# Splitting the value weights earlier in the opening of a one-core attention and gated-feed-forward kernel

## The chip, the core and the metric

The kernel runs on one core of one Trainium2 chip. The metric is device time in microseconds (us) of one launch: 689.45 us before the change, the median of three runs (689.45 to 689.49).

The engines are named as the profile names them. PE is the matrix engine (PEld is its weight load, which runs beside the matmuls), DVE the vector engine, ACT the scalar engine, POOL the general-purpose engine, and SP the engine that issues nearly all loads and stores.

## The reference, cut to what matters

`x` holds 2048 tokens of 448 channels. All weight products use the layer-normed tokens `xn`:

```python
xn = _layernorm(x, axis=-1)
return x + _A_ref(xn, A_wq, A_wk, A_wv, A_wo, A_beta) + _B_ref(xn, B_w_gate, B_w_up, B_w_down)
```

`_A_ref` is attention with 16 heads of 28 channels over four segments of 512 tokens. It projects queries, keys and values (`xn @ wq`, `xn @ wk`, `xn @ wv`), attends causally inside a segment, mixes in a read of a memory that is summed over the earlier segments, and multiplies by `wo`. `_B_ref` is `(sigmoid(xn @ w_gate) * (xn @ w_up)) @ w_down` with 1792 inner channels. What the change touches is only the very beginning: the layer norm of the first 512 tokens and the product `xn @ wv` for them.

## The kernel before, in words

**Precision.** Every operand of a large product is split into a high part, rounded to the matmul type by an ACT copy, and a low part, which is the rest. The low part of weights in the opening is made by POOL, and that of tokens by DVE. One product is a sum of eleven matmuls over pairs of parts.

**Blocks and tiles.** The 2048 tokens stand in four blocks of 512, and a block in four tiles of 128. `acc[b]` holds the raw tokens of a block; `xs[b]` holds the normed tokens turned (channels on partitions): parts 0 to 2 are the high parts of three groups of 128 channels, part 3 has the last 64 channels, high in one half and low in the other, and parts 4 to 6 are the low parts. So that part 3 can hold both, the last 64 channels are repeated in columns 448 to 511 of the normed tile `xn`; in the first block ACT makes these repeated channels (L324). `wv[0]` to `wv[3]` are the high value weights, `wv[4]` to `wv[7]` the low ones.

**The opening (L407 to L501).** For each of the first four tiles, the same steps follow each other:

- `statistics`: three DVE instructions, mean and variance (L294 to L296).
- `root`: one small ACT square root (L301).
- `normalised`: on DVE a reciprocal, two small corrections (L308 to L311) and the normed tile (L320), then the repeated channels on ACT (L324).
- `turn_high`: four PE transposes (L95) into a PSUM bank and one ACT copy into the high parts (L97). The first three transposes need only L320; the fourth also reads the repeated channels.
- `turn_low`: two DVE subtractions that make the low parts (L102, L103).

Beside them, `split_v(t)` makes `wv[t]` by an ACT copy of the raw weights (L431) and `wv[4 + t]` by a POOL subtraction (L432). `value_terms(b, t, pv, terms, n0, n1)` issues the matmuls n0 to n1 of the eleven of one tile (L335), and `store_values` copies the sum out of PSUM on ACT (L339). `fill(n)` issues n small matmuls of no use but to keep PE busy (L445), each of which the trace counts as two; ten more of them (L442) stand at the very start.

`EARLY[0]`, the order of the eleven matmuls for the first two tiles, begins with three high by high (they need `wv[0]`, `wv[1]` and `wv[2]`), then three with the tokens' low parts, then one with part 3 and `wv[3]`, then three with `wv[4]` to `wv[6]`, and last the one with `wv[7]`.

**What sets the order.** Around the opening stands

```python
with tc.tile_pool(name="front", bufs=2) as sb, tc.manual_schedule(engines=FRONT):
```

with PE, ACT and DVE in `FRONT`: the instructions of these three engines run in just the order in which the code lists them. POOL and SP are ordered by the framework. Each engine takes its instructions in order; one that waits holds back all behind it. SP issues the loads in this order: tokens of tile 0 (L409), of tile 1 (L410), first half of the value weights (L411, `wv[0]` and `wv[1]`), second half (L412, `wv[2]` and `wv[3]`), tokens of tiles 2 and 3 together (L413), then weights of queries and keys and the next block's tokens.

After the opening come the queries and keys of each block (L355), the memory updates, and the long part in which feed-forward matmuls and attention alternate in an order written out by hand for PE and SP.

Of the kernel before, what the change touches and what calls it, by code (L numbers as in the profile page):

```python
# [17 lines left out]
D = 448  # L18
# [33 lines left out]
EARLY = [HIGH + LOW_X + [(3, 3)] + LOW_W + [(3, 7)], HIGH + LOW_W + LOW_X + [(3, 3), (3, 7)]]  # L52
# [9 lines left out]
def kernel(  # L62
# [28 lines left out]
    def transpose_high(pt, src, dst, t):  # L91

        tok = slice(t * P, (t + 1) * P)
        for c in range(4):
            T.transpose(pt[:, c * P:(c + 1) * P], src[:, c * P:(c + 1) * P], ident)  # L95
        p3 = pt.rearrange("p (c n) -> p c n", c=4)
        A.activation(dst[:, 0:4, tok], p3, AF.Copy)  # L97
        return p3

    def transpose_low(p3, dst, t):  # L100
        tok = slice(t * P, (t + 1) * P)
        V.tensor_sub(dst[:, 4:7, tok], p3[:, 0:3], dst[:, 0:3, tok].bitcast(F32))  # L102
        V.tensor_sub(dst[64:, 3, tok], p3[64:, 3], dst[64:, 3, tok].bitcast(F32))  # L103
# [11 lines left out]
    def bank(name, tag):  # L115
        return ps.tile([P, L], F32, name=name, tag=tag, bufs=banks[tag])
# [32 lines left out]
    def four_k(dtype, name):  # L149
        return mid.tile([P, 2, L], dtype, name=name, tag="4k", bufs=4)  # L150
# [125 lines left out]
    with tc.tile_pool(name="front", bufs=2) as sb, tc.manual_schedule(engines=FRONT):  # L276
# [11 lines left out]
        def statistics(b, t0, steps):  # L288

            stats = sb.tile([P, steps, 6], F32, name=f"stats{steps}")  # L290
            mv = sb.tile([P, steps, 2], F32, name=f"mv{steps}")
            vh = sb.tile([P, steps], F32, name=f"vh{steps}")
            for t in range(steps):
                V.bn_stats(stats[:, t, :], acc[b][:, t0 + t, :])  # L294
                V.bn_aggr(mv[:, t, :], stats[:, t, :])
            V.tensor_scalar(vh, mv[:, :, 1], EPS, -0.5, op0=ALU.add, op1=ALU.mult)  # L296
            return mv, vh

        def root(vh):
            y = sb.tile([P, vh.shape[1]], F32, name=f"y{vh.shape[1]}")  # L300
            A.activation(y, vh, AF.Sqrt, scale=-2.0)  # L301
            return y

        def rstd(mv, vh, y):

            steps = vh.shape[1]
            tm = sb.tile([P, steps], F32, name=f"tm{steps}")
            V.reciprocal(y, y)  # L308
            if steps == 1:
                V.tensor_scalar(tm, y, y, vh, op0=ALU.mult, op1=ALU.mult)  # L310
                V.tensor_scalar(y, tm, 1.5, y, op0=ALU.add, op1=ALU.mult)  # L311
            else:
                V.tensor_mul(tm, y, y)
                V.tensor_mul(tm, tm, vh)
                V.scalar_tensor_tensor(y, tm, 1.5, y, op0=ALU.add, op1=ALU.mult)
            return [(mv[:, t, 0:1], y[:, t:t + 1]) for t in range(steps)]

        def normalise(b, t, mean, y):
            xn = sb.tile([P, 512], F32, name="xn")
            V.tensor_scalar(xn[:, :D].rearrange("p (m h c) -> p h m c", h=H, c=4),  # L320
                              acc[b][:, t, :].rearrange("p (h m c) -> p h m c", h=H, c=4), mean, y,
                              op0=ALU.subtract, op1=ALU.mult)
            if b == 0:
                A.activation(xn[:, D:], xn[:, 384:D], AF.Copy)  # L324
            else:
                G.tensor_copy(xn[:, D:], xn[:, 384:D])
            return xn
# [4 lines left out]
        def value_terms(b, t, pv, terms, n0=0, n1=len(TERMS)):  # L332
            for n in range(n0, n1):
                a, w = terms[n]
                T.matmul(pv[:, :D], xs[b][:, a, t * P:(t + 1) * P], wv[w],  # L335
                         start=n == 0, stop=n == len(TERMS) - 1)

        def store_values(b, t, pv):
            A.activation(vst[:, t, :, :DH], pv[:, :D].rearrange("p (h d) -> p h d", d=DH), AF.Copy)  # L339
            if t == NT - 1:  # L340
                nc.sync.dma_start(vd[b], vst.rearrange("p t h d -> p t (h d)"))
# [65 lines left out]
        raw = [four_k(F32, "wv_raw") for _ in range(2)]  # L407
        raw = [r.rearrange("p a n -> p (a n)")[:, :2 * D] for r in raw]
# [2 lines left out]
        nc.sync.dma_start(raw[0], w_v[:, :2 * D])  # L411
        nc.sync.dma_start(raw[1], w_v[:, 2 * D:])  # L412
        nc.sync.dma_start(acc[0][:, 2:4, :], x[2 * P:L, :].rearrange("(t p) d -> p t d", p=P))  # L413
        raw = [raw[t // 2][:, t % 2 * D:(t % 2 + 1) * D] for t in range(4)]
        nc.sync.dma_start(stage[:, 0:2, :], w_qk[0:2].rearrange("c p n -> p c n"))
        nc.sync.dma_start(stage[:, 2:4, :], w_qk[2:4].rearrange("c p n -> p c n"))
        raw_qk = [stage[:, c, :] for c in range(4)]
# [8 lines left out]
                nc.sync.dma_start(gate[32 * j:32 * j + 32], beta[j::HG].partition_broadcast(32))  # L426
        G.memset(vst[:, :, :, DH:], 1.0)
        A.activation(gate_n, vst[:, 0, :NG, DH], AF.Sqrt)

        def split_v(t):  # L430
            A.activation(wv[t], raw[t], AF.Copy)  # L431
            G.tensor_sub(wv[4 + t], raw[t], wv[t].bitcast(F32))  # L432
# [10 lines left out]
        def fill(n):  # L443
            for _ in range(n):
                T.matmul(warm[:, :P], ident, ident, start=True, stop=True)  # L445

        def turn_high(t):
            p3[t] = transpose_high(bank("pt", "s"), xn[t], xs[0], t)

        def turn_low(t):  # L450
            transpose_low(p3[t], xs[0], t)

        def normalised(t):
            xn[t] = normalise(0, t, *rstd(*st[t], y[t])[0])
# [2 lines left out]
        st[0] = statistics(0, 0, 1)  # L457
        y[0] = root(st[0][1])
        normalised(0)
        st[1] = statistics(0, 1, 1)  # L460
        y[1] = root(st[1][1])
        turn_high(0)
        fill(5)
        split_v(0)
        split_v(1)
        normalised(1)
        split_v(2)
        split_v(3)
        turn_low(0)
        turn_high(1)  # L470
        st[2] = statistics(0, 2, 1)
        y[2] = root(st[2][1])
        turn_low(1)
        normalised(2)
        st[3] = statistics(0, 3, 1)
        pv = [bank("pv", "p") for _ in range(2)]
        for t in range(2):
            value_terms(0, t, pv[t], EARLY[0], 0, 7)
        value_terms(0, 0, pv[0], EARLY[0], 7)
        store_values(0, 0, pv[0])  # L480
        y[3] = root(st[3][1])
        turn_high(2)
        value_terms(0, 1, pv[1], EARLY[0], 7)
        store_values(0, 1, pv[1])
# [3 lines left out]
        pv = bank("pv", "p")  # L488
# [345 lines left out]
```

## Time and profile before

| what | value |
|---|---|
| median of three runs | 689.45 us (689.45 to 689.49) |
| the profiled execution's own time | 689.46 us |
| its span, first to last instruction | 687.7 us |
| PE busy | 681.7 us, 99% of the span |
| DVE busy | 567.4 us, 83% |
| ACT busy | 342.6 us, 50% |
| POOL busy | 151.3 us, 22% |

The profile is of one execution. A row of the timeline gives the start in us from the span's start, the duration in us, the engine, the line in the kernel, the operation and what it writes and reads; "x4" at its end says that four neighbouring instructions were merged, and the duration then goes from the first start to the last end. A row of the chain of waits names the work that, followed back from the end, was late at that time. Matmuls are pipelined, so several overlap, and a busy PE is not PE at its peak.

### The profile page before, as it was taken

How to read it: one execution, taken by the hardware profiler on the slowest of the kernel's cores; microseconds unless marked ns; L12 is line 12 of the kernel's file. 1: busy time of each engine (PE TensorE's matmuls, PEld its weight loads, DVE VectorE, ACT ScalarE, POOL GpSimd, SP SyncE). 2: the span in 40 equal slices, each digit the busy share in tenths (PEclk: the TensorE clock that was granted, in tenths of full speed). 3: DMA queues.
4: the chain of work that ended last, by engine and by line, in shares of the span. 5: the costliest groups of instructions: out<-in, count | busy, mean ns of one | idle time of the engine just before them, and what ended most of it. 6: DMA issues, size and time to landing. Idle time of an engine off the chain costs nothing.

```text
span 687.7 us, 10438 instructions
## 1 busy us (share of the span) xinstructions
PE 681.7 (99%) x3594; PEld 566.6 (82%) x3594; DVE 567.4 (83%) x994; ACT 342.6 (50%) x563; POOL 151.3 (22%) x349
## 2 busy tenths in 40 slices
PE   8999999999999999999999999999999999999997
PEld 7898888778878787787878878787787878878897
DVE  6765795767788988998898989989898899889863
ACT  4837555343554555543655446454653565446320
POOL 3500020101223222232332222322322322222000
PEclk9999999999999999999999999999999999999999
DMA  7446556696233323243223252314333332423342
GB/s 267 181 150 238 198 214 242 249 330 174 71 94 92 80 86 86 56 128 112 56 64 107 57 141 56 109 47 116 82 94 77 96 71 64 95 79 95 95 153 106
DMA packets 45796, 84.37 MB, mean 123 GB/s; under 512 B 6320, under 2 KB 20400, under 8 KB 45232
## 3 DMA queue, kind: packets, MB, share of 16 engines
q1 hardware_dynamic: 42736, 76.37, 35.8%
q0 software_dynamic: 3008, 7.34, 4.9%
q8 instruction: 28, 0.46, 0.3%
q14 instruction: 24, 0.20, 0.1%
HBM read 51.05 MB, written 32.64 MB: 122 GB/s over the span
## 4 chain that ended last, share of the span: by engine, by line
PE 70%; DVE 14%; issue 9%; POOL 4%; DMA 1%; ACT 1%; SPq 0%; POOLq 0%; ACTq 0%
PE pgu L247 26%; PE pd L173 13%; PE pp L355 10%; PE po L771 5%; PE pv L335 5%; PE st L612 3%; PE pa L687 3%; DVE mx L629 3%; DVE w L666 2%; POOL w L627 2%; DVE acc L174 2%; PE pmm L383 2%; PE n L401 2%; DVE hh L259 1%; DVE mx L633 1%
## 5 line engine op out<-in xcount | busy, mean ns | idle before, releaser
L247 PE MATMUL pgu<-xs,wgu 128*128 128x512 f32 x1232 | 304.1, 394 | 0.0
L247 PEld LDWEIGHTS pgu<-xs,wgu 128*128 128x128 f32 x1232 | 228.2, 188 | 47.4 <-issue 2.2
L173 PE MATMUL pd<-wdn,hh 128*128 128x448 f32 x672 | 156.0, 367 | 0.0
L627 POOL TENSOR_SCALAR_AFFINE_SELECT w<-w 128x256 f32<-128x256 f32 (+1 forms) x160 | 81.2, 509 | 236.4 <-ACT w L616 183.6
L173 PEld LDWEIGHTS pd<-wdn,hh 128*128 128x128 f32 x672 | 122.5, 188 | 12.3 <-issue 0.6
L667 ACT ACTIVATE w<-w 128x1024 f32<-128x1024 f32 (+1 forms) x96 | 87.3, 915 | 65.0 <-DVE w L666 64.2
L666 DVE TENSOR_TENSOR w<-w,mb 128x1024 f32<-128x1024 f32 (+1 forms) x96 | 98.9, 1045 | 0.1
L616 ACT ACTIVATE w<-st 128x512 f32<-128x512 f32 x128 | 74.9, 590 | 45.3 <-PE st L612 44.9
L629 DVE TRANSPOSE_TENSOR_REDUCE mx<-w 128x32 f32<-128x1024 f32 x64 | 79.0, 1235 | 17.0 <-POOL w L627 17.0
L355 PE MATMUL pp<-xs,wqk 128*128 128x512 f32 x308 | 77.7, 401 | 0.0
L174 DVE TENSOR_TENSOR acc<-pd,acc 128x448 f32<-128x448 f32 x112 | 67.1, 599 | 1.2 <-PE pd L173 1.1
L355 PEld LDWEIGHTS pp<-xs,wqk 128*128 128x128 f32 x308 | 56.8, 188 | 13.4 <-issue 2.4
L258 ACT ACTIVATE hh<-sg 128x512 fp32r<-128x512 f32 x56 | 35.2, 628 | 56.4 <-DVE sg L256 49.3
L612 PE MATMUL st<-qk 84*128 84x128 f32 (+3 forms) x256 | 61.9, 312 | 0.0
L255 ACT ACTIVATE sg<-pgu 128x512 f32<-128x512 f32 x56 | 33.2, 594 | 49.4 <-PE pgu L247 49.2
L612 PEld LDWEIGHTS st<-qk 84*128 84x128 f32 x256 | 47.6, 189 | 6.9 <-ACT w L616 0.3
L656 DVE STREAM_TRANSPOSE mb<-top 128x1024 f32<-128x1024 f32 x32 | 39.8, 1242 | 10.5 <-POOL top L653 10.1
L362 DVE TENSOR_TENSOR qk<-pp,qk 128x512 fp32r<-128x512 f32 x28 | 19.3, 688 | 29.8 <-ACT e L360 23.7
L259 DVE SCALAR_TENSOR_TENSOR hh<-sg,hh 128x512 fp32r<-128x512 f32 x56 | 38.7, 691 | 2.6 <-ACT hh L258 2.4
L335 PE MATMUL pv<-wv,xs 128*128 128x448 f32 x176 | 39.6, 376 | 0.4 <-DVE xs L102 0.3
L687 PE MATMUL pa<-w,vv 128*32 128x128 f32 (+3 forms) x512 | 39.7, 436 | 0.2
L256 DVE SCALAR_TENSOR_TENSOR sg<-sg,pgu 128x512 f32<-128x512 f32 x56 | 37.3, 665 | 1.8 <-PE pgu L247 1.6
(100 smaller groups left out, 640.6 us busy)
## 6 DMA issues: line engine op xcount, KB each, us to landing
qk<-qd SPq DMA_DIRECT2D x192, 112.0 KB
qd<-qk SPq DMA_DIRECT2D x28, 512.0 KB
raw<-in_w_ffn SPq DMA_DIRECT2D x14, 512.0 KB
vd<-vst SPq DMA_DIRECT2D x4, 1024.0 KB
vv<-vd SPq DMA_DIRECT2D x16, 256.0 KB
od<-w POOLq DMA_DIRECT2D x16, 256.0 KB, 3.8
sums<-od SPq DMA_DIRECT2D x32, 128.0 KB
out<-acc SPq DMA_DIRECT2D x16, 224.0 KB
```

The costliest lines, as they stand in the source:

```text
L173: T.matmul(pd[:, :D], l, r, start=n == 0, stop=n == len(mms) - 1)
L174: V.tensor_add(acc[b][:, t, :], pd[:, :D], acc[b][:, t, :])
L247: T.matmul(dst, wgu[f][:, w, side * P:(side + 1) * P], xs[b][:, a, :], start=n == 0, stop=n == len(TERMS) - 1)
L335: T.matmul(pv[:, :D], xs[b][:, a, t * P:(t + 1) * P], wv[w], start=n == 0, stop=n == len(TERMS) - 1)
L355: T.matmul(pp, wqk[c][:, w, :], xs[b][:, a, :], start=n == 0, stop=n == len(TERMS) - 1)
L612: T.matmul(st[:, at:at + L - kb * P], self.qk[:KS, 1, h, kb * P:(kb + 1) * P], self.qk[:KS, 0, h, kb * P:], start=True, stop=True)
L616: A.activation(w, st, AF.Copy)
L627: G.affine_select(d, d, pattern=pattern, base=0, channel_multiplier=-1, compare_op=ALU.is_ge, fill=MASK)
L629: V.tensor_reduce(mx[:, 16 * (n - 1):16 * (n + 1)], w3[:, n // 2, :2 * L].rearrange("p (b n) -> p b n", n=32), axis=mybir.AxisListType.X, ...
L666: V.tensor_sub(w, w, m)
L667: A.activation(w, w, AF.Exp, scale=SCALE)
L687: T.matmul(pa[32 * j:32 * j + 32, kb * P:], self.vv[:, kb, 32 * j:32 * j + 32], self.pairs[j // 2].block(j % 2, kb), start=kb == 0, stop=k ...
```

## The change

All lines stand in the opening. The split of the first value weights (`split_v(0)`) goes to just behind the first tile's normed tokens and repeated channels, ahead of the second tile's square root. `split_v(1)` and `split_v(2)` go ahead of the second tile's norm. Three of the first tile's value matmuls go ahead of the second tile's transposes, with two fill matmuls behind them where there were five ahead of them. The remaining matmuls of the first two tiles are dealt out anew between the turns of the second and the third tile. The two PSUM banks for them are taken earlier. The line that names the four slices of the raw weights moves, which issues nothing; loads stay as they are.

```diff
         st[0] = statistics(0, 0, 1)
         y[0] = root(st[0][1])
         normalised(0)
+        split_v(0)
         st[1] = statistics(0, 1, 1)
         y[1] = root(st[1][1])
         turn_high(0)
-        fill(5)
-        split_v(0)
         split_v(1)
+        pv = [bank("pv", "p") for _ in range(2)]
+        split_v(2)
+        value_terms(0, 0, pv[0], EARLY[0], 0, 3)
+        fill(2)
         normalised(1)
-        split_v(2)
         split_v(3)
         turn_low(0)
         turn_high(1)
         st[2] = statistics(0, 2, 1)
         y[2] = root(st[2][1])
+        value_terms(0, 0, pv[0], EARLY[0], 3, 10)
         turn_low(1)
         normalised(2)
+        value_terms(0, 1, pv[1], EARLY[0], 0, 3)
+        value_terms(0, 0, pv[0], EARLY[0], 10)
+        store_values(0, 0, pv[0])
         st[3] = statistics(0, 3, 1)
-        pv = [bank("pv", "p") for _ in range(2)]
-        for t in range(2):
-            value_terms(0, t, pv[t], EARLY[0], 0, 7)
-        value_terms(0, 0, pv[0], EARLY[0], 7)
-        store_values(0, 0, pv[0])
         y[3] = root(st[3][1])
+        value_terms(0, 1, pv[1], EARLY[0], 3, 7)
         turn_high(2)
         value_terms(0, 1, pv[1], EARLY[0], 7)
         store_values(0, 1, pv[1])
```

More of the change, by code (lines that the diff above doesn't have):

```diff
@@ L413 @@
         nc.sync.dma_start(acc[0][:, 2:4, :], x[2 * P:L, :].rearrange("(t p) d -> p t d", p=P))
-        raw = [raw[t // 2][:, t % 2 * D:(t % 2 + 1) * D] for t in range(4)]
         nc.sync.dma_start(stage[:, 0:2, :], w_qk[0:2].rearrange("c p n -> p c n"))
@@ L428 @@
         A.activation(gate_n, vst[:, 0, :NG, DH], AF.Sqrt)
+        raw = [raw[t // 2][:, t % 2 * D:(t % 2 + 1) * D] for t in range(4)]
         def split_v(t):
```

## The prediction, made before the changed kernel was run

> **What bounds the kernel now.** I read the page first, then PE's waits, then the chain of waits for the opening, and last each engine's timeline there. In the table of PE's waits the columns are the wait's total in us, how often, and the longest.
>
> ```profile
> span 687.7 us, 10438 instructions
> PE 681.7 (99%) x3594; PEld 566.6 (82%) x3594; DVE 567.4 (83%) x994; ACT 342.6 (50%) x563; POOL 151.3 (22%) x349
> ```
>
> ```profile
> PE warm L442 <- POOL ident masks.py:199: 1.5, 1, 1.5
> PE pt L95 <- DVE xn L320: 0.4, 1, 0.4
> PE pv L335 <- DVE xs L102: 0.3, 1, 0.3
> ```
>
> These three are all of PE's waits in the whole span, and the two that lie near the change are the turn of tile 1 and a value product. From the third tile on PE has work without a gap. So the time is the moment at which this unbroken stretch starts, plus the matmuls behind that moment, which are the same before and after. The chain of waits says what sets the moment (start, duration, what was late):
>
> ```profile
> 2.67 7.19 DMA acc<-in_x
> 9.88 0.64 DVE stats L294
> ...
> 10.94 0.56 DVE xs L102
> 11.54 0.29 DVE xs L103
> 11.86 0.17 DVE y L308
> ...
> 14.11 0.20 ACT y L301
> 14.31 0.49 ACT xs L97
> 14.85 1.48 PE pv L335 x6
> ...
> 44.63 8.81 PE pv L335 x44
> ```
>
> The reader is to see a chain that starts with a load: the tokens of tiles 2 and 3 land at 9.88. DVE takes their statistics, then makes tile 1's low parts (10.94, L102), then norms tile 2, then takes tile 3's statistics; ACT makes tile 3's root (14.11) and only then tile 2's high parts, and with these PE starts at 14.85. The last row gives the pace of value matmuls where nothing waits: 8.81 / 44 = 0.20 us each.
>
> **The change part by part.** It moves three things on engines whose order is the code's own: the weight splits on ACT, matmuls on PE, and fills on PE. It adds or removes no load, no store and no DVE instruction. First, the order on ACT, which decides:
>
> ```profile
> 6.08 0.26 ACT L324 ACTIVATE xn<-xn 128x64 f32<-128x64 f32 x1 [1.34 <-DVE xn L320]
> 7.02 0.20 ACT L301 ACTIVATE y<-vh 128x1 f32<-128x1 f32 x1 [0.69 <-DVE vh L296]
> 7.15 0.60 ACT L97 ACTIVATE xs<-pt 128x512 fp32r<-128x512 f32 x1
> 7.64 1.03 ACT L431 ACTIVATE wv<-wv_raw 128x448 fp32r<-128x448 f32 x2
> 8.57 0.25 ACT L324 ACTIVATE xn<-xn 128x64 f32<-128x64 f32 x1
> 8.74 1.05 ACT L431 ACTIVATE wv<-wv_raw 128x448 fp32r<-128x448 f32 x2
> 9.70 0.58 ACT L97 ACTIVATE xs<-pt 128x512 fp32r<-128x512 f32 x1
> ```
>
> Before, ACT idles from 6.34 to 7.02, and it is into this gap that the first weight copy is put. It fits only if the raw weights have landed. When do they? Three rows answer, from SP's timeline, SP's waits and the instructions of L432:
>
> ```profile
> 7.59 0.53 SPq L423 DMA_DIRECT2D wqk_raw<-in_w_qk  x1
> ```
>
> ```profile
> SPq L423 <- DMA wv_raw<-in_w_v: 1.1, 1, 1.1
> ```
>
> ```profile
> L432 POOLq EVENT_SEMAPHORE  x2: 17/17/17, 7.6 to 8.7; - x2
> L431 ACT ACTIVATE wv<-wv_raw x4: 562/566/579, 7.6 to 9.2; 128x448 fp32r<-128x448 f32 x4
> ```
>
> SP stood 1.1 us for the first half of the value weights and went on at 7.59; POOL, idle until then, passed its two semaphores at 7.6 and 8.7. So the first half lands at about 7.59 and the second at about 8.7. Loads do not change, so they land then again, and the moved copy, behind the repeated channels that end at 6.34, **adds a wait of 1.25 us** on ACT. Queued behind it are tile 1's root and tile 0's high parts, which before ran at 7.02 and 7.15, in the very time of that wait. DVE waits for the first to norm tile 1, PE for the second. Step by step on ACT: copy 0 runs 7.60 to 8.17 (0.57, the row of L431). ACT starts the next 0.47 behind a copy (two copies in 1.05, less 0.57 = 0.48): root at 8.07 to 8.27, tile 0's high parts 0.13 later (7.15 - 7.02) at 8.20 to 8.80, copy 1 at 8.69 (7.64 - 7.15 = 0.49 later), copy 2 at 9.17 to 9.74. Against before, the root is 1.05 later.
>
> DVE goes on from the root as it did before:
>
> ```profile
> 7.26 0.16 DVE L308 RECIPROCAL y<-y 128x1 f32<-128x1 f32 x1 [0.27 <-ACT y L301]
> 8.01 0.51 DVE L320 TENSOR_SCALAR xn<-acc,mv,y 128x448 f32<-128x448 f32 x1
> 8.45 0.55 DVE L102 TENSOR_TENSOR xs<-pt,xs 128x384 fp32r<-128x384 f32 x1
> 9.03 0.29 DVE L103 TENSOR_TENSOR xs<-pt,xs 64x128 fp32r<-64x128 f32 x1
> ```
>
> Its last step, L103, ended before at 9.32, and DVE then idled 0.56 for the load at 9.88. Now everything is 1.05 later: L320 at 9.06, L102 at 9.50, L103 at 10.08, and the next instruction 0.32 behind it (11.86 - 11.54): tile 2's statistics at 10.40 in place of 9.88. The 0.56 of cover is used up, and 0.5 is left over. By DVE alone, tile 1's low parts come at 10.40 + 1.06 (10.94 - 9.88) = 11.46.
>
> PE, for the same step. Its rows, with a transpose batch that waited for nothing at 13.28:
>
> ```profile
> 1.53 4.64 PE L442 MATMUL warm<-ident 128*128 128x128 f32 x20 [1.53 <-POOL ident masks.py:199]
> 6.10 1.01 PE L95 MATMUL pt<-ident,xn 128*128 128x128 f32 x4
> 6.95 1.28 PE L445 MATMUL warm<-ident 128*128 128x128 f32 x10
> 8.58 0.66 PE L95 MATMUL pt<-ident,xn 128*128 128x128 f32 x4 [0.35 <-DVE xn L320]
> 11.56 1.88 PE L335 MATMUL pv<-wv,xs 128*128 128x448 f32 x8 [0.28 <-DVE xs L102]
> 13.28 0.63 PE L95 MATMUL pt<-ident,xn 128*128 128x128 f32 x4
> ```
>
> Before, tile 1 was turned at 8.58. Now three value matmuls stand ahead of it, and the third needs copy 2: 9.74 + 0.06 (a matmul at 11.56 follows L102's end at 11.50), so it starts at 9.80 and gives PE free at 10.00. The two fills are four of the trace's instructions of 1.28 / 10 = 0.13 at most: to about 10.50. The turn takes 0.63 to its end, 11.13; the ACT copy 0.04 and 0.58 more, 11.75; DVE can start tile 1's low parts at about 11.78. That is later than DVE's own 11.46, so it sets the step: 11.78 in place of 10.94, **0.8 us late**. Of this, 0.5 comes from the late root and 0.3 from the matmuls and fills ahead of the turn.
>
> From there to the start of the stretch, DVE and ACT hold the same instructions in the same order as before (tile 1's low parts, tile 2's norm, tile 3's statistics and root, tile 2's high parts), so 0.8 is carried on, 14.85 to 15.65, if nothing else becomes late. The rest of the dealing out lies beside this chain. On PE, seven matmuls from about 10.9 end at 12.3, three of tile 1 at 12.9, and the first tile's last one needs `wv[7]`:
>
> ```profile
> 8.29 4.57 POOL L432 TENSOR_TENSOR wv<-wv_raw,wv 128x448 fp32r<-128x448 f32 x4 [5.92 <-ACT wv L431]
> ```
>
> ACT's row for tile 2's repeated channels is this:
>
> ```profile
> 13.23 0.26 ACT L324 ACTIVATE xn<-xn 128x64 f32<-128x64 f32 x1 [2.08 <-DVE xn L320]
> ```
>
> POOL starts right behind copy 0, now 0.05 earlier, and is done at about 12.8, in time. So the first tile's sum stands at about 13.3, and ACT comes to its store only behind tile 2's repeated channels, at 13.23 + 0.8 + 0.25 = 14.3: 1.0 of cover. Four more matmuls end by 13.9, ahead of tile 2's turn at 14.1; the last four follow and end by 15.3, ahead of 15.65. Each of these costs nothing while that cover stands. The two banks taken earlier had no user before them, and moving the line of slices costs nothing. POOL's and SP's other work here is passed by nothing.
>
> **The sum:** 689.46 (the profiled execution) + 0.8 = 690.26; the median stands 0.01 below the profiled execution, so **690.25 us**, 0.12% more. Bounds: nothing where all is hidden (689.45), and 1.05, the whole lateness of the root, where DVE's idle time covers none of it (690.5).
>
> **The clock.** The first 20 instructions took 4.64 / 20 = 0.23 us each, the ten at 6.95 only 0.13, so PE sped up by nearly two after some 5 us of work. The change opens a gap there: PE is free at 7.11 and starts its first value matmul behind tile 0's high parts at 8.86, 1.75 us later, then waits again for each weight copy. [...] No run here shows what a half-busy stretch does.
>
> **The rivals.**
>
> *Slow clock (slower).* If the thin stretch from 7.1 on slows PE again to the rate of the rows at 1.53, value matmuls take 0.40 in place of 0.20. Say it lasts as long as at the start, 5.4 us (1.53 to 6.95), from the first value matmul at 8.9 to 14.3. Then the third matmul ends at 10.2, the four fill instructions at 11.1 (0.23 each), the turn of tile 1 at 12.1 (1.01, as at 6.10), 1.0 later than reckoned; of the fifteen matmuls ahead of tile 2's turn, six are done by 14.3 and nine more by 16.1, 1.0 later than that turn would otherwise be due. In all 0.8 + 1.0 + 1.0 = 2.8, 692.25. It decides as soon as it lasts past 10, when it first reaches the turn. Between 0.8 and 2.8 I take the middle, 1.8: 691.25. For it: five fills go and two come back later. Against it: PE's gap of 1.75 is short beside the 5.4 that the speed-up took. 0.15.
>
> *Weights in time (no change).* If the first half lands before 6.34, copy 0 uses ACT's gap, the root is not late, and DVE is again covered by its 0.56; the load at 9.88 sets all, 689.45. Against: the three rows at 7.59. Partly in time (landing by 7.1) leaves 0.3, 689.75. 0.12.
>
> *Later order (either side).* ACT, DVE and POOL are ordered by the framework behind the opening, and another opening may deal their work otherwise. PE's waits show nothing to gain there, so 0.04 for a gain of 1.5 or more (688) and 0.05 for a loss of 1.5 or more (691).
>
> *It does not do what it says*: ACT order is the code's, and I see no way around the copy's wait; it has no share of its own.
>
> That leaves 0.64 for the forecast, from 689.95 (only DVE's 0.5) to 690.5. A gain beyond noise has no cause inside the opening, since the load at 9.88 and the DVE order behind it stay.
>
> **How the numbers follow.** This kernel's measurement can tell about 0.2%, 1.4 us, from no change. Forecast (0.64) and weights in time (0.12) lie within it; slow clock (0.15) and a later loss (0.05) are slower by more; a later gain (0.04) is faster. So 0.04 faster, 0.76 same, 0.20 slower. For the range: the forecast's own, plus weights in time, plus the nearer half of the slow clock gives 0.84: 689.3 to 691.3.
>
> **What would show it.** In the changed kernel's ACT rows, copy 0 starts at 7.6 with an idle time before it put down to the load, the root of tile 1 runs near 8.07, and tile 2's statistics start near 10.4, not 9.88. Tile 1's low parts start near 11.8; the chain still goes through tile 3's root and tile 2's high parts, and PE's stretch starts near 15.65. Wrong, if the copy starts at 6.3; if statistics still start at 9.88; if value matmuls between 10.5 and 13.7 stand 0.4 apart; or if the stretch starts 0.8 later and the end does not move with it.

## The result, and the profile after

The changed kernel takes 690.88 us (median of 22 runs, 689.09 to 692.31) against 689.51 us before (22 runs, 689.38 to 690.04): a ratio of 1.0016 over all runs (1.0020 by the medians alone), 95% interval 1.001 to 1.0023. It is slower, by 1.37 us, just inside the 0.2% that the prediction had called no change. More telling than the median is the spread: 3.2 us, where the kernel before has 0.7. Each run also lists the mean clock granted to PE, as a share of full speed. In seven of the 22 runs it is 0.999 or 1.000, as in all 99 runs of the kernel before that were timed beside the experiments; these take 689.09 to 690.32, median 689.58. In the other fifteen it is 0.995 to 0.998, and they take 690.38 to 692.31, median 691.05. So there are two kinds of execution, and the profiled one (691.05 us, span 689.4) is of the second.

PE's waits in its first 16 us (total, times, longest) show the gap that the change opened, where before there were 0.4 and 0.3:

```profile
PE pv L335 <- ACT xs L97: 1.7, 1, 1.7
PE warm L442 <- POOL ident masks.py:199: 1.5, 1, 1.5
PE pt L95 <- DVE xn L320: 0.2, 1, 0.2
```

ACT's timeline shows where it comes from:

```profile
6.10 0.26 ACT L324 ACTIVATE xn<-xn 128x64 f32<-128x64 f32 x1 [1.34 <-DVE xn L320]
7.23 0.58 ACT L431 ACTIVATE wv<-wv_raw 128x448 fp32r<-128x448 f32 x1 [0.87 <-DMA wv_raw<-in_w_v]
7.71 0.19 ACT L301 ACTIVATE y<-vh 128x1 f32<-128x1 f32 x1
7.81 0.58 ACT L97 ACTIVATE xs<-pt 128x512 fp32r<-128x512 f32 x1
...
11.85 0.60 ACT L97 ACTIVATE xs<-pt 128x512 fp32r<-128x512 f32 x1 [1.82 <-PE pt L95]
```

The first weight copy stands 0.87 us for its load, and the root (7.71, before 7.02) and tile 0's high parts (7.81, before 7.15) stand behind it. The weights landed at 7.22, though, not at 7.59. The last row is the larger loss: tile 1's high parts come at 11.85, 2.15 us later than before, and they waited for PE. PE's timeline, and then its stretches (length, busy time of PE, PEld, DVE, ACT and POOL, each with its number of instructions, granted clock, DMA share, GB/s):

```profile
6.12 0.66 PE L95 MATMUL pt<-ident,xn 128*128 128x128 f32 x4 [0.20 <-DVE xn L320]
8.44 1.67 PE L335 MATMUL pv<-wv,xs 128*128 128x448 f32 x3 [1.66 <-ACT xs L97]
9.90 1.06 PE L445 MATMUL warm<-ident 128*128 128x128 f32 x4
10.76 1.06 PE L95 MATMUL pt<-ident,xn 128*128 128x128 f32 x4
```

```profile
8.00:9.00 1.00, 0.56 (x2) 0.29 (x2) 0.89 (x4) 1.00 (x3) 1.00 (x2) 0.97 1.04 366
9.00:10.00 1.00, 1.00 (x3) 0.78 (x4) 0.97 (x3) 1.00 (x3) 1.00 (x2) 0.50 1.03 398
...
12.00:13.00 1.00, 1.00 (x6) 0.90 (x5) 0.52 (x1) 0.54 (x2) 0.46 (x1) 0.82 1.06 388
```

The clock is the third number from the end of a row. It is 0.97 from 8 to 9, so half speed began 0.06 before 9.00; 0.50 from 9 on; and 0.82 from 12 to 13, so half speed lasted 0.36 into it: from 8.94 to 12.36, 3.4 us. Tile 1's turn took 1.06 us in it, and the four fill instructions 1.06 where kernel 1 below takes 0.61. The turn at 6.10 in the kernel before had been as slow (1.01), because PE had not yet sped up there: its small matmuls come 0.11 apart only in the fills from 6.95 on. That slow time at the very start doesn't show in the clock of the rows, which is 1.00 there. The chain of waits confirms the path:

```profile
1.74 5.47 DMA wv_raw<-in_w_v
7.21 0.02 issue
7.23 0.58 ACT wv L431
...
10.96 0.85 PE pt L95 x4
11.82 3.33 PE pv L335 x15
15.14 0.44 PE pt L95 x4
15.58 2.28 PE pv L335 x10
```

Before, the chain began with the tokens of tiles 2 and 3 and ran over DVE. Now it begins with the value weights and ends on PE. The third tile's first six matmuls, with which the unbroken stretch begins, have their weights loaded behind tile 2's high parts:

```profile
16.38 1.11 PEld L335 LDWEIGHTS pv<-wv,xs 128*128 128x128 f32 x6 [0.36 <-ACT xs L97]
```

That is 16.38, 1.53 later than the 14.85 of before. The 44 value matmuls that the chain of before has at 44.63 stand at 46.17 here, still 1.54 later, and the profiled execution's span is 1.7 longer: nearly all of the loss is made in the opening and carried through to the end.

### The profile page after: what moved, and what is told of

The parts are those of the page before. It is cut to its first block, busy times and chain, and to the rows that moved or that the text cites. A ratio compares the mean times of both kernels' runs of the same rounds, so it can differ in the third digit from the quotient of the medians.

```text
span 689.4 us, 10426 instructions
## 1 busy us (share of the span) xinstructions
PE 682.1 (99%) x3588; PEld 567.0 (82%) x3588; DVE 567.4 (82%) x994; ACT 342.7 (50%) x563; POOL 152.0 (22%) x349
## 4 chain that ended last, share of the span: by engine, by line
PE 71%; DVE 13%; issue 9%; POOL 4%; ACT 1%; DMA 1%; POOLq 0%; SPq 0%; ACTq 0%
PE pgu L247 26%; PE pd L173 13%; PE pp L355 10%; PE pv L335 5%; PE po L773 5%; PE st L614 3%; PE pa L689 3%; DVE mx L631 3%; DVE w L668 2%; POOL w L629 2%; DVE acc L174 2%; PE pmm L383 2%; PE n L401 1%; DVE hh L259 1%; DVE mx L635 1%
```

## The experiments

Three theories are told apart. The **clock** theory says that the thin work of PE lets the granted clock fall for a while in most runs, and that this is most of the loss. The **wait** theory is the prediction's: the copy that waits for its weights makes the root late. The **dealing** (or POOL) theory came up with the first four runs: the new order of value matmuls brings PE to products whose low weights POOL has not made yet. Each kernel was timed 11 times, against 33 runs of the kernel before on the same chip (medians 689.46 to 689.52, mean clock 0.999 or 1.000 in every one). "Drop" below means a run with a mean clock of 0.998 or less.

**1. The gap filled.** The changed kernel with

```diff
         turn_high(0)
+        fill(6)
         split_v(1)
```

> The changed kernel with six fills put back right behind tile 0's transposes, so that PE stays busy from about 7.0 to 8.5 us. Clock theory (the thin stretch makes the granted clock drop for one window of 3.4 us in most runs, and that is most of the loss): no drop in any run, mean clock 0.999 in all, times within about 0.7 us of each other around 689.6, the level of the changed kernel's runs without a drop (689.1 to 690.3). Wait theory (the copy that waits for the raw weights makes the root late, and that is the loss): no gain from fills, 690.3 to 690.9 with the spread of the changed kernel.

Measured: 689.92 (689.17 to 690.64), no drop in 11 runs. Six fills, which compute nothing, take 0.96 us off the changed kernel's median: the clock is shown to be the larger part. But the median stays 0.4 above before and the spread is 1.5, so something that varies is left. Its profile (690.05 us) is the forecast's path without the clock:

```profile
1.72 5.52 DMA wv_raw<-in_w_v
7.25 0.02 issue
7.27 0.58 ACT wv L431
7.84 0.09 ACT y L301
7.94 0.49 ACT xs L97
8.43 0.04 issue
8.47 1.40 PE pv L335 x3
9.88 0.44 PE warm L445 x4
10.32 0.45 PE pt L95 x4
...
11.42 0.56 DVE xs L102
...
15.32 1.47 PE pv L335 x6
```

Tile 1's low parts start at 11.42 (before 10.94) and the stretch at 15.32 (before 14.85): 0.47 late, where the prediction had 0.8 for weights that land 0.34 later than here.

**2. The wait taken away, the gap left.** The changed kernel with

```diff
         normalised(0)
-        split_v(0)
...
         turn_high(0)
+        split_v(0)
```

> The changed kernel with the first weight copy back behind tile 0's high parts on ACT, so that the second tile's root no longer waits for the load; fills as in the changed kernel. Wait theory: back to 689.5 in all runs. Clock theory: PE still idles from 7.0 to about 8.2 and is thin after that, so the clock still drops in a good part of the runs, median 690.2 to 690.9, runs without a drop at 689.4 to 689.6.

Measured: 690.83 (689.94 to 692.17), seven drops in 11. Without any wait for the weights the loss is the same: the wait theory fails as the main cause. The four runs without a drop (689.94 to 690.29) lie at least 0.34 above what the clock theory expected of them (689.4 to 689.6): a second hint at something else.

**3. Only the gap.** The kernel before with

```diff
         turn_high(0)
-        fill(5)
         split_v(0)
```

> The kernel before without its five fills, nothing else changed. Clock theory: PE idles from about 7.1 to 8.6 as in the changed kernel, so the clock drops in a part of the runs, fewer than in the changed kernel since PE is dense from 8.6 on; those runs lie about 1 us higher, the others at 689.5; median 689.5 to 690.5 and a wider spread than before's 0.7. Wait theory: no wait was added, 689.5 and the spread of before.

Measured: 690.22 (689.45 to 691.52), eight drops in 11; I had expected fewer than in the changed kernel. The five fills of the kernel before are worth 0.7 us.

**4. Neither gap nor wait.** Edits 1 and 2 together.

```diff
         normalised(0)
-        split_v(0)
...
         turn_high(0)
+        split_v(0)
+        fill(6)
         split_v(1)
```

> The changed kernel with the first copy back behind tile 0's high parts and six fills behind tile 0's transposes: of the change only the new dealing out of the value matmuls and the two fills ahead of tile 1's turn are left. Both theories: 689.5 to 689.9 with a spread under 0.7; clock theory says the same as for the kernel with fills alone or up to 0.4 less, wait theory 0.8 to 1.4 less than that kernel.

Measured: 689.96 (689.86 to 690.40), no drop. The spread is gone, but 0.44 stays, and every run is at least 0.34 above the median of before. The median is just above the range that both theories gave; what is left of the change is the dealing and the two late fills.

**6. The two late fills taken out as well** (the kernel of 4 without `fill(2)`).

```diff
         value_terms(0, 0, pv[0], EARLY[0], 0, 3)
-        fill(2)
         normalised(1)
```

> The kernel with copy back and six fills, now without the two fills between the first three value matmuls and tile 1's transposes. Fill theory (the two fills make tile 1's turn late by 0.45 us, and that is why the kernel with both stays at 689.96): 689.5. Dealing theory (PE comes to the first tile's products with the low weights before POOL has made them, with tile 1's products queued behind): 689.85 to 690.0, PE waiting for POOL near 11.6 us as before the cut. Clock theory: no drop with either.

Measured: 689.95 (689.85 to 690.04), as the dealing theory had it. The fills are not it. PE's waits have a new row, and the chain runs through POOL:

```profile
PE pv L335 <- POOL wv L432: 0.5, 1, 0.5
```

```profile
8.31 0.44 POOL wv L432
...
10.66 1.14 POOL wv L432
11.81 0.04 issue
11.85 1.08 PE pv L335 x4
```

The first tile's seven matmuls from index 3 end with three on `wv[4]` to `wv[6]`. The third comes to PE before POOL is done with `wv[6]` at 11.81, and tile 1's products, which need nothing of POOL, are queued behind it. The old order had them ahead. The profiled run of the changed kernel has no such row: there tile 1's turn is later still, and POOL is done in time.

**5. Only the early copy.** The kernel before with `split_v(0)` moved up to where the change puts it, all else as it was.

```diff
         normalised(0)
+        split_v(0)
...
         fill(5)
-        split_v(0)
         split_v(1)
```

> The kernel before with one thing of the change: the first weight copy (and its POOL subtraction) right behind the first tile's repeated channels; matmuls and the five fills as before. Wait theory (ACT stands for the weights, which land anywhere between 6.1 and 7.6 us from one execution to the next): a spread over 0.8 us, from 689.1 where they land by 6.3 to 690.0 where they land at 7.6, median 689.5 to 689.9. Dealing theory (what is left over beside the clock comes from the new order of the value matmuls): 689.5 or less in every run, since that order is the old one. Clock theory: no drop, mean clock 0.999 or more in all runs.

Measured: 689.53 (689.00 to 689.70, and one run with a drop at 691.58). The median is the wait theory's and the spread nearly so (0.7 without the drop, where over 0.8 was expected), the dealing theory (never above 689.5) is too low, and the clock theory missed the one drop. The spread is centred on before, and four runs of 11 take 689.24 or less, below every run of before. So the early copy alone is a gamble that can win, which the prediction had ruled out. What it can win: POOL's subtractions start 0.08 behind the copy's end. In the profiled execution (689.60, not one of the fast ones) that copy ended at 7.68, and they ran from 7.76 to 12.38, before from 8.29 to 12.86.

**7. The weights loaded first.** The kernel of 1 with the load of the first half of the weights put ahead of that of tile 1's tokens.

```diff
-        nc.sync.dma_start(acc[0][:, 1, :], x[P:2 * P, :])
         nc.sync.dma_start(raw[0], w_v[:, :2 * D])
+        nc.sync.dma_start(acc[0][:, 1, :], x[P:2 * P, :])
```

> The changed kernel with six fills and one load moved: the first half of the value weights ahead of tile 1's tokens. Wait theory: the copy finds its weights at 6.3 and the spread of the kernel with fills alone goes; 689.0 to 689.3 if tile 1's tokens still land by 6.0; if they land at 7, statistics, root and turn of tile 1 are late by 1 us and the time is 689.8 to 690.3. Dealing theory: POOL starts 0.7 to 1.3 us earlier, so its weights are in time, 689.0 to 689.3 as well.

Measured: 689.42 (689.16 to 689.71), no drop. The copy ran at 6.21 without a wait, and the spread fell from 1.5 to 0.6. Its chain still has the two late fills and tile 1's turn (low parts at 10.90, stretch at 14.80), so it only comes level with before, 0.1 above what was expected.

**8. The tokens loaded first.** The kernel before with the load of tiles 2 and 3 ahead of that of the second half of the weights, the copies of that half behind tile 2's statistics, and matmuls dealt out to suit.

```diff
-        nc.sync.dma_start(raw[1], w_v[:, 2 * D:])
         nc.sync.dma_start(acc[0][:, 2:4, :], x[2 * P:L, :].rearrange("(t p) d -> p t d", p=P))
+        nc.sync.dma_start(raw[1], w_v[:, 2 * D:])
...
         normalised(1)
-        split_v(2)
-        split_v(3)
         turn_low(0)
         turn_high(1)
         st[2] = statistics(0, 2, 1)
+        split_v(2)
         y[2] = root(st[2][1])
+        split_v(3)
         turn_low(1)
...
```

> A try at a version that beats both: the kernel before with the tokens of tiles 2 and 3 loaded ahead of the second half of the value weights, the copies of that half behind tile 2's statistics, and the matmuls dealt out so that those with the second half come late. If the chain from the tokens' landing at 9.9 us sets the start of PE's unbroken stretch, tile 2's statistics start at 9.3 (behind tile 0's low parts) and the stretch 0.3 to 0.6 earlier: 688.9 to 689.2. If POOL's four subtractions, done at about 12.9, set it as well, nothing is gained: 689.4 to 689.6. No clock drop, five fills stand where they stood.

Measured: 689.43 (689.38 to 689.51). Nothing, although tile 2's statistics did start at 9.26. The rows of DVE and of POOL say where the 0.6 went:

```profile
11.99 1.04 DVE L320 TENSOR_SCALAR xn<-acc,mv,y 128x448 f32<-128x448 f32 x1
```

```profile
11.63 1.14 POOL L432 TENSOR_TENSOR wv<-wv_raw,wv 128x448 fp32r<-128x448 f32 x1
```

The same norm takes 0.51 elsewhere. Here it begins in the middle of POOL's last subtraction and ends 0.26 behind it (13.03 against 12.77). The same stands in two other profiles: in kernel 3 it takes 1.02 from 12.02, POOL ending at 12.79, and in kernel 6 it takes 0.70 from 12.47, POOL ending at 12.91; each time the norm ends 0.25 or 0.26 behind POOL. In the changed kernel and in kernels 1, 5 and 12 it is tile 1's norm that begins during POOL's first subtraction; it takes 0.58 or 0.59 and ends 0.25 behind that one. Why the norm takes longer beside POOL, none of these rows shows.

**11. POOL's last subtraction done by DVE**, behind tile 3's statistics, with the two matmuls that need it moved behind the first six of tile 2; else as 8 (`order` is the order in which 8 has the eleven matmuls).

```diff
-        split_v(3)
+        A.activation(wv[3], raw[3], AF.Copy)
...
+        V.tensor_sub(wv[7], raw[3], wv[3].bitcast(F32))
         normalised(3)
...
         value_terms(0, 2, pv, EARLY[1], 0, 6)
+        for t in range(2):
+            value_terms(0, t, first[t], order, 10)
+            store_values(0, t, first[t])
...
```

> The kernel with tiles 2 and 3 loaded first, now with the last of POOL's four subtractions done by DVE behind tile 3's statistics, and the two matmuls that need it behind the first six of tile 2. POOL theory: nothing of POOL's runs any more when DVE norms tile 2 at about 12.0, so this takes 0.51 us and not 1.04, the stretch starts near 14.2, and the time is 688.8 to 689.1. If the 1.04 had another cause: it stays at 1.04 and the time at 689.4.

Measured: 689.44 (689.34 to 689.72). Half a hit. The norm takes its plain time once nothing runs on POOL, whose third subtraction ended at 11.86, and the chain shows PE's next start earlier:

```profile
12.17 0.51 DVE L320 TENSOR_SCALAR xn<-acc,mv,y 128x448 f32<-128x448 f32 x1
```

```profile
14.40 1.88 PE pv L335 x8
```

It starts at 14.40, not 14.74 as in kernel 8, but with eight matmuls in place of six: the two that I had moved behind cost 2 x 0.20, which eats up the 0.34 that was gained. My expectation had left them out of the sum.

**9. Early copy and early weights.** The kernel before with the diffs of 5 and 7.

> The kernel before with the first weight copy early on ACT and the first half of the value weights loaded ahead of tile 1's tokens, so that the copy need not wait; matmuls and five fills as before. POOL theory (before is held by POOL's last subtraction of the value weights as much as by the tokens: tile 2's norm on DVE ends 0.25 us after that subtraction ends): POOL is done at about 11.8 and not 12.86, tile 2's norm takes 0.51 us and ends at 12.6 to 13.1, time 688.9 to 689.3. If only the tokens' landing at 9.9 us holds it: 689.4 to 689.5.

Measured: 689.02 (688.91 to 689.75), ratio 0.9994 (0.9985 to 1.0003). Seven of 11 runs lie between 688.91 and 689.03, below all 33 of before (689.34 at least); the interval still holds 1. This is the version that the runs point to: 0.5 us faster where it works. None of the seven was profiled. The profiled execution (689.75) is the slowest of the eleven, and shows one way in which it fails; DVE's idle time before tile 1's statistics is

```profile
6.70 0.63 DVE L294 BATCH_NORM_STATS2 stats<-acc 128x6 f32<-128x448 f32 x1 [0.65 <-DMA acc<-in_x]
```

so tile 1's tokens, now second, can be 0.65 late.

**10. The change mended.** The kernel of 7 without the two late fills (the diff of 6).

> The changed kernel with six fills behind tile 0's transposes, without the two ahead of tile 1's, and with the first half of the value weights loaded ahead of tile 1's tokens. POOL theory: with the low weights early PE does not wait for POOL, and the new dealing of the matmuls costs nothing: 688.9 to 689.2, as the kernel before with early copy and early load. Dealing theory taken by itself (the new order costs 0.4 whatever POOL does): 689.3 to 689.5.

Measured: 689.32 (688.91 to 690.31). Four runs of 11 take 688.91 to 689.03, the level of kernel 9's good runs, so with early low weights the new dealing need not cost anything. The other seven are later; in the profiled one (689.91), tile 1's statistics waited 0.90 for their tokens, and PE did not wait for POOL. The median lies in the range of the dealing theory, but that theory allowed no run at 689.0. The load order brings its own gamble, and what made the other late runs late was not seen.

**12. Half the gap filled.** The changed kernel with `fill(3)` in place of the six of kernel 1.

```diff
         turn_high(0)
+        fill(3)
         split_v(1)
```

> The changed kernel with three fills behind tile 0's transposes, half of what covers the gap. Clock theory: how full a window of 3.4 us has to be decides; 44% and 47% busy windows were followed by a drop, one of 62% was not. Three fills add about 0.75 us, 22% of a window, so drops in a few runs at most (0 to 4 of 11), median 689.9 to 690.4. If any gap of over 0.9 us is enough for a drop, 6 to 9 of 11 runs with one, median 690.7 to 690.9.

Measured: 689.88 (689.46 to 691.80), one drop in 11, as the clock theory had it (whose median, 689.9 at least, was 0.02 too high).

What decides is told by the traces. The twenty matmuls at the very start are the same in all kernels: they begin 0.21 us apart, and from some moment on PE's small matmuls come 0.11 apart. This speed-up comes at 5.5 in the profile of the changed kernel, half speed begins 3.41 later, at 8.94, and ends 3.41 after that; in kernels 2 and 3 the three moments lie 3.41 apart as well. So I count PE's busy time in the 3.41 us behind the speed-up. First the changed kernel, then kernels 3 and 2, where half speed followed; then kernels 5 and 9, where the clock stayed at 1.00:

```profile
5.53:8.94 3.41, 1.55 (x9) 0.85 (x8) 2.28 (x8) 1.97 (x6) 1.05 (x1) 1.00 1.02 367
8.94:12.35 3.41, 3.41 (x12) 3.12 (x13) 2.06 (x6) 1.59 (x5) 3.41 (x4) 0.50 1.05 405
```

```profile
5.63:9.04 3.41, 1.51 (x12) 1.09 (x12) 2.93 (x10) 2.33 (x7) 0.84 (x1) 1.00 1.02 361
9.04:12.45 3.41, 3.41 (x12) 3.03 (x11) 3.11 (x10) 1.35 (x4) 3.41 (x4) 0.50 1.05 403
```

```profile
5.27:8.69 3.42, 1.71 (x11) 1.01 (x9) 2.94 (x10) 1.97 (x6) 0.49 (x1) 1.00 0.95 307
```

```profile
5.80:9.21 3.41, 2.03 (x17) 1.65 (x16) 2.43 (x9) 1.91 (x6) 1.45 (x2) 1.00 1.01 367
9.21:12.62 3.41, 3.41 (x19) 3.05 (x20) 3.11 (x10) 1.85 (x5) 3.17 (x3) 1.00 1.04 400
```

```profile
6.06:9.47 3.41, 1.96 (x16) 1.73 (x16) 2.33 (x8) 2.04 (x7) 1.61 (x2) 1.00 0.99 345
```

1.51, 1.55 and 1.71 busy (44, 45 and 50% of the stretch) were followed by half speed, 1.96 and 2.03 (57 and 60%) were not; counted so, these stand in place of the expectation's 44, 47 and 62%. The length of the gap does not tell them apart: PE's longest wait there was 1.47 in kernel 2, with a drop, and 1.45 in kernel 9, without one.

In the other nine profiles the stretch behind the speed-up is 2.6 busy or more, and the clock stays at 1.00. Kernel 12's is one of these: its speed-up came at 7.4, and the stretch from there is 94% busy, so this one execution tests nothing. The speed-up came between 4.7 (kernel 8) and 7.6 (kernel 7). I take it from this that the same thin work can fill one such stretch in one execution and be split over two in another, and that this is why one kernel drops in some runs and not in others; it is a guess, for no kernel was profiled both ways.

## Why the prediction was right or wrong

**Direction and size.** Slower, and within 0.2%, were right; 690.25 was 0.63 too low, and it is a time that hardly any run takes: it lies between the two kinds, 689.6 and 691.05. That the range held is in part luck: the larger part of the loss came from a rival that had been given 0.15, and the wait that the forecast was made of is the smaller part.

**The wait on ACT: right in its mechanism, mis-sized in its one input.** Root, high parts, DVE's statistics and PE's turn came late in the order that was worked out. "Loads do not change, so they land then again" was the step that failed. The first half of the weights landed at 7.22 in the profiled run and at 7.59 in that of before, and in kernel 3 by 6.12, when the SP load that had stood for it went out with no wait:

```profile
6.12 0.98 SPq L423 DMA_DIRECT2D wqk_raw<-in_w_qk  x1
```

The working, fed with kernel 1's 7.25, gives 0.8 - 0.34 = 0.46; kernel 1 measured 0.47. Of the signs that the prediction named, the wait before the copy, the late root (7.71) and the late statistics of tile 2 (10.10) are in the changed kernel's profile, each 0.3 to 0.4 early; the chain through tile 3's root and tile 2's high parts is in kernel 1's profile and not in the changed kernel's, and the stretch starts at 15.32 there and at 16.38 in the changed kernel.

**The slow clock: right price, wrong chance.** It was priced at 1.8 in all, as the middle of two bounds, and given 0.15. It came in 15 of 22 runs and makes them 691.05 - 689.51 = 1.54 slower. The middle was lucky, but the step behind it held: a drop from 8.94 to 12.36 reaches little more than tile 1's turn, which the prediction had at 1.0 later. By the chains that turn ends at 11.82 in the changed kernel and at 10.77 in kernel 1, 1.05 apart. With the weights at 7.25 the prediction's own working so gives 0.46 + 1.0 = 1.46.

The failed step is the one that weighed the gap of 1.75 against the 5.4 us that the speed-up took at the start. The profiled gap was 1.66 and enough, since a stretch of 3.4 us that was only 45% busy sufficed. And the 5.4 was one execution's: the speed-up at 4.7 in kernel 8 and at 7.6 in kernel 7 makes it about 3 and 6.

That PE stays fast across such a gap, which the forecast's sum takes for granted, no run had shown. In the three profiles with a drop (the changed kernel, kernels 2 and 3) the clock fell to 0.50 for 3.41 us and did so 3.41 or 3.42 behind the speed-up, which came anywhere from 4.7 to 7.6 over all profiles.

**"Each of these costs nothing while that cover stands": not shown wrong in the changed kernel, but wrong as a statement on the dealing.** Kernels 4 and 6 show 0.44 and 0.49 as soon as the turn of tile 1 is no longer late. The two late fills, part of the 0.3 given to what stands ahead of that turn, cost nothing where PE waits for POOL anyway: kernel 6 without them gained nothing on kernel 4.

**"A gain beyond noise has no cause inside the opening": wrong.** In the kernel before, two chains end together: the tokens' landing, and POOL's last subtraction. DVE's norm of tile 2 takes its plain time there and ends at 13.13; POOL is done at 12.86, so a norm that ends 0.25 behind it, as in kernels 3, 6 and 8, would have ended at 13.11.

```profile
12.62 0.51 DVE L320 TENSOR_SCALAR xn<-acc,mv,y 128x448 f32<-128x448 f32 x1
```

In kernel 3, where DVE and POOL do what they did before, the tokens had landed by 9.29, and the same norm ends at 13.04, only 0.09 earlier:

```profile
12.02 1.02 DVE L320 TENSOR_SCALAR xn<-acc,mv,y 128x448 f32<-128x448 f32 x1
```

With the tokens early nothing moves (kernels 3 and 8); where POOL starts earlier as well, up to 0.5 us is gained (kernels 5 and 9). That would also be why the seven runs of the changed kernel without a drop are only 0.07 slower in the median, and one is 0.3 below the lowest of before's 22: the early copy wins back what its wait costs.

What stays open: no execution with this gain was profiled, neither of the changed kernel, whose 689.09 is explained by kernels 1 and 5 and not seen, nor of kernels 5, 9 and 10. The seven runs have a median 0.34 below that of kernel 1, which has no drop either; whether they are the ones whose weights came early was not shown. Whether transposes count like other matmuls in the busy share was not tried, nor why the loads' landing moves by over 1 us between executions.

## What to carry to other kernels

Before moving work out of a gap that fill work covers, add up how busy the matrix engine is over every stretch of some 3.4 us: here half speed followed at 50% and less and did not at 57% and more. Where the first of them started differed from execution to execution (4.7 to 7.6 us), and the changed kernel's thin place brought the drop in 15 runs of 22: its time became a matter of luck. A copy that waits for a load (0.87 us here, with the root and the high parts behind it) belongs behind whatever in-order work others need, or its load belongs further ahead. And when removing a bound gains nothing, look for an instruction that suddenly takes longer: here a norm took 1.04 us in place of 0.51 while POOL was at work, and no row of waits said so.

## What the runs showed of the hardware that was not expected

- The granted clock fell to 0.50 for 3.41 us after a stretch as long in which PE was 44 to 50% busy, with idle gaps of 1.66, 1.47 and 1.82 us at the longest (the changed kernel, kernels 2 and 3), and did not after 57 and 60% (kernels 9 and 5).
- PE's speed-up at the start, where all kernels have the same twenty matmuls, came between 4.7 and 7.6 us in different executions.
- A DVE norm of 128x448 that takes 0.51 us took 0.58 to 1.04 when it began during a POOL subtraction, and ended 0.25 to 0.26 us behind it. In the kernel before, where it began 0.24 ahead of POOL's end, it took its plain 0.51.
- The same 448 KB load landed by 6.12 us in one execution (kernel 3) and at 7.59 in another (the kernel before), with the same order of loads and the second load behind it (L413) issued at 2.67 in both.
